# Memory reused tile by tile behind an attention stage, with one expert's weights split ahead of its first products

## The chip, the core and the metric

The kernel runs on one core of a Trainium2 chip. A core has TensorE (PE, matrix products), VectorE (DVE), ScalarE (ACT), GpSimd (POOL) and SyncE (SP), which here only issues transfers. The engines run beside each other and wait for each other through semaphores; each executes its own list of instructions in order. SBUF is the memory they work in, PSUM the accumulators that PE writes, and DRAM is reached by DMA. The metric is the device time of one execution, in microseconds, as the median of three runs.

## The reference

Attention over 8 batches, 8 heads, 576 positions and head dimension 64, with a causal window of 32 for four heads and a dilated one (every fourth position, 32 of them) for the other four; its 4608 x 512 output x then goes through a mixture of experts with one expert for each row:

```python
attn = softmax(where(mask, q @ k.T / 8, -1e9)) @ v      # window 32 | dilation 4
x = attn.transpose(0, 2, 1, 3).reshape(4608, 512)
logits = x @ w_gate                                     # 8 experts
e = argmax(logits, axis=1)
out[i] = gate[i] * (relu(x[i] @ w1[e[i]]) @ w2[e[i]])   # w1 512x1024, w2 1024x512
```

## The kernel before

**Attention** goes in 36 steps of 128 rows, nine for each of four pairs of batches; a step n runs scores of tile n, the weighted sum (`st_av`) of tile n-2, the transposes of tile n-3 (`st_xt`, copied by `st_xcopy`) and the logits of three tiles at a time (`st_logits`, `st_keep`). Its accumulators are the PSUM pool `psa` with tags X, S0, S1, T, O and L; its SBUF pools are `fix`, `ap`, `sp` and `late`. The ring buffers `qkr` and `vr` for q, k and v lie in `fix`. Finished rows are written to a DRAM table `x_d`.

**Routing** (`route(m)`) runs once for each pair of batches, as short pieces that the steps pull from a list (`on_pe`, `off_pe`). It transposes the logits (`turn`), takes the best expert of each row, counts with three small products (`rank`) how many rows each expert had before, and selects each row's place (`select`): a block of 128 slots and a slot in it. For the first three pairs POOL scatters the row numbers into three DRAM tables, 27 scatters in all; `read_table` reads these back into `t_in`. For the last pair the table is made on chip: for each of its nine tiles DVE writes `b1` (which of 320 blocks, L562) and `s1` (which slot, times the row number, L554), six buffers of each, and PE multiplies them into one accumulator `tb` (`enter`, L573). The sum of `tb` and the three tables is `row_i`, the row number for each slot of each expert; with it POOL gathers rows of `x_d`. In the listing POOL adds the three tables (L674, L675), and three DVE operations make `row_i` from them and `tb` (L656, L660, L661; the trace has the last as L437).

**The first expert** is partly ahead. Its first 256 rows come from the first two pairs, are gathered and transposed during attention, and `early_layer1` makes hidden blocks 0 to 3 of its first layer in attention's accumulators S0 and S1 while the last routing runs. Every weight unit (128 x 1024) is loaded into one of three `raw` buffers and split (`split_unit`): ACT writes the high part (L720), DVE the rest (L721). Units 0 to 3 (first layer) are ready early; units 4 to 6 (second layer) are loaded early and split later.

**Behind attention** `att.close()` releases its pools, and `ps`, `ph`, `pw1`, `pw2`, `px1`, `pd` and `py` are laid over their memory. A tile of such a pool waits for every user of the pools it is laid over. Then come `layer1` for hidden blocks 4 to 7, each 12 matmuls of 256 columns with ACT's `h` (L911) and DVE's (L912) behind it, and the split of units 4 to 7 (unit 7 is loaded only now, as a `raw` buffer must be free). From here the order of all engines is written out by hand: `keep_rows` (`row_i` to DRAM), the gathers of the first expert's other two blocks r0 and r1 and of the next expert's, the loads of the next expert's units (`bring`), `layer2` of the first expert's two blocks, `r0.prep_x` (four transposes, L970, of the gathered rows), `r0.layer1` (L1005), and so on for seven more experts. Up to that point from step 35 on the order is a scheduler's: it lists, for each engine, what is ready by its own estimates of time, first what stands first in the program, or what is marked with high priority.

Of the kernel before, what the change touches and what calls it, by code (L numbers as in the profile page):

```python
# [9 lines left out]
F32 = mybir.dt.float32  # L10
# [15 lines left out]
NE = 8  # L26
# [38 lines left out]
C_ID, C_TRI, C_REV, C_C0, C_NEW, C_IO, C_ATT = np.cumsum(  # L65
    [0, P, P, NE, NE, NE * NT, P]
).tolist()
C_ONE, C_BASE, C_THR, C_PU, C_D, C_P, C_BK, C_FIRST, C_WSTEP, C_UP, C_AT, C_ALL = (
    C_ATT + np.cumsum([0, P, NE, NTHR, NE, DBLK, DBLK, NBK, 2 * NE + 1, 2 * NE, 1, DBLK])
).tolist()  # L70


def _constants():
    c = np.zeros((P, C_ALL), np.float32)
    c[:, C_ID : C_ID + P] = np.eye(P)
    c[:, C_TRI : C_TRI + P] = -np.tril(np.ones((P, P)))
    c[:, C_ONE : C_ONE + P] = 1.0
    c[:, C_REV : C_REV + NE] = np.arange(NE, 0, -1)
    c[0, C_C0 : C_C0 + NE] = np.arange(NE) * CAP
    c[:, C_BASE : C_BASE + NE] = np.arange(NE) * CAP  # L80
    c[:, C_THR : C_THR + NTHR] = SLOTS + P * np.arange(NTHR)
    c[:, C_PU : C_PU + NE] = np.arange(NE)[None, :] * P + np.arange(P)[:, None]
    c[:, C_D : C_D + DBIG] = np.arange(DBIG)
    c[:, C_D + DBIG : C_D + DBLK] = np.arange(DTAIL)
    c[:, C_FIRST : C_FIRST + 2 * NE] = np.tile(np.arange(NE) * CAP + SLOTS, 2)
    c[:, C_FIRST + 2 * NE] = 2.0**20
    c[:, C_WSTEP : C_WSTEP + 2 * NE] = np.diff(np.append(np.tile(np.arange(NE), 2), NE - 1)) * 8 * P
    c[:, C_UP] = np.arange(P) // TAIL
    own = np.repeat(np.arange(P)[:, None], DBLK, 1)
    own[:, DBIG:] %= TAIL  # L90
    c[:, C_P : C_P + DBLK] = own
    c[:, C_AT : C_AT + DBLK] = own * (NBK + 1)
    c[:, C_NEW : C_NEW + NE * NT] = np.arange(NE * NT) % NT != 0
    c[:, C_IO : C_IO + P] = np.arange(P)
    c[:, C_BK : C_BK + NBK] = P * np.arange(NBK)
    row = (
        DUMMY
        + np.arange(NPR)[None, :, None] * S2
        + np.arange(NT)[None, None, :] * P
        + np.arange(P)[:, None, None]  # L100
    )
    tok = row[:, :-1].astype(np.int32)
    end = row[:, -1].astype(np.float32) - LAST

    t, p, w = np.meshgrid(np.arange(NT), np.arange(P), np.arange(KB), indexing="ij")
    q, k = P * t + p, P * t + p // QB * QB - W + w

    def near(n):
        return (k >= 0) & (q >= k) & (q - k < W) & (q // n == k // n)

    def blocks(m):
        m = m.reshape(-1, NB, QB, KB).transpose(2, 0, 1, 3).reshape(QB, -1)
        return np.where(m, 0.0, -BIG)


    mask = np.zeros((P, QB + NT * NB * KB), np.float32)
    mask[:QB, : QB + 3 * NB * KB] = np.concatenate(
        [np.eye(QB), blocks(near(S)[[0, S // P, 1]])], axis=1
    )
    mask[QB:] = np.concatenate([np.eye(QB), blocks(near(CLS))], axis=1)  # L120
    mask = mask.astype(mybir.dt.np(BF16))
    slots = np.repeat(np.arange(P, dtype=np.int32)[:, None], NBK, 1)
    return dict(cst=c, tok=tok, end=end, slots=slots, mask=mask, zero=np.zeros((DUMMY, XP), np.float32))
# [39 lines left out]
def attention_moe_kernel(ctx, tc, qk, v, wg, w, cst, tok, end, slots, mask, zero, out):  # L163
# [33 lines left out]
    t_in = [late.tile([P, NBK], I32, name=f"t_in{i}") for i in range(3)]  # L197

    NRQ, NRV = 6, 6
    qkr = fix.tile([P, NRQ, QK], F32, name="qkr")  # L200
    vr = fix.tile([P, NRV, VC], F32, name="vr")
    rows_i = fix.tile([P, NPR - 1, NT], I32, name="rows_i")
    rows_f = fix.tile([P, NT], F32, name="rows_f")
    wgz = fix.tile([P, 4, 32], F32, name="wgz")
# [228 lines left out]
    def on_pe(f, *a, late=False):  # L433
        side.append((2 if late else 1, lambda: f(*a)))

    def off_pe(f, *a, **k):
        side.append((0, lambda: f(*a, **k)))  # L437
# [15 lines left out]
    def hold(on):  # L453
        held_[0] = on
# [19 lines left out]
    def route(m, then=None, after=None):  # L474
# [25 lines left out]
        def small(name, shape=(P, NT, NE), dt=F32):  # L500
            return sp.tile(list(shape), dt, name=name, bufs=1)
# [7 lines left out]
        pos, blk_i, plc_i, at_i = [  # L509
            small(n, (P, NT), I32) for n in ("pos", "blk_i", "plc_i", "at_i")  # L510
        ]
        wide, pay = [small(n, (P, NT)) for n in ("wide", "pay")]
        load = small("load", (P, NT), I32)
        many = small("many", (P, NT, XP - DM))
        posf = small("posf", (P, NT))
# [35 lines left out]
        def mark(t):  # L551
            s1 = sp.tile([P, P], F32R, name="s1", bufs=6)
            b1 = sp.tile([P, NBK], F32R, name="b1", bufs=6)
            v.tensor_scalar(  # L554
                s1,
                ca[:, C_IO - C_TRI : C_IO + P - C_TRI],
                plc[:, t : t + 1],
                pay[:, t : t + 1],
                op0=ALU.is_equal,
                op1=ALU.mult,  # L560
            )
            v.tensor_scalar(  # L562
                b1, cc[:, C_BK - C_ATT : C_BK + NBK - C_ATT], blk[:, t : t + 1], None, op0=ALU.is_equal
            )
            hot[t] = s1, b1
# [47 lines left out]
        )  # L613
        if m == NPR - 2:
            off_pe(hold, True)
        on_pe(rank, late=True)
        off_both(
            select,
            lambda: v.tensor_reduce(
# [23 lines left out]
        else:  # L643
            off_both(
                lambda: v.tensor_copy(blk, blk_i),
                lambda: v.tensor_copy(plc, plc_i),
                lambda: v.tensor_tensor(pay, rows_f, plc, op=ALU.subtract),
            )
            off_pe(lambda: v.tensor_tensor(crun, crun, cs[:, :, NT - 1], op=ALU.add))
            for lo in range(0, NT + 3, 3):  # L650
                for t in range(lo, min(lo + 3, NT)):
                    off_pe(mark, t)
                if lo:
                    on_pe(enter, range(lo - 3, lo), late=True)
            off_pe(
                lambda: v.tensor_scalar(  # L656
                    scr, box["tb"], 0.0, float(LAST), op0=ALU.is_gt, op1=ALU.mult
                )
            )
            off_pe(lambda: v.tensor_tensor(scr, box["tb"], scr, op=ALU.add))  # L660
            off_pe(v.tensor_tensor, row_i, t_in[0], scr, op=ALU.add)  # L661
        if after:
            after()

# [6 lines left out]
    def add_tables(rows, n):  # L671

        t0, t1, t2 = [t[:, :n] for t in t_in]
        nc.gpsimd.tensor_tensor(t0, t0, t1, op=ALU.add)  # L674
        nc.gpsimd.tensor_tensor(rows, t0, t2, op=ALU.add)  # L675
# [451 lines left out]
    def at(n, f, *a):  # L1127
        todo.setdefault(n, []).append(lambda: f(*a))
# [2 lines left out]

    def read_all():
        read_table(NBK)
        add_tables(t_in[0], NBK)

    def early_fetch():
        def fetch():
# [27 lines left out]
        at(8 + 2 * u, early_split, u)  # L1165
    for u in range(4, 7):
        at(total + u - 4, early_load, u)

    def early_layer1(f):
        n = first.ns  # L1170
# [6 lines left out]
    def go(f, n):  # L1177
        if 0 <= n < total:
            f(n)
# [5 lines left out]
    def step(n):  # L1185
# [36 lines left out]
        pull_off()  # L1222
        go(st_logits, n - 4)
        go(st_keep, n - 4)
        pull_pe(late=True)
        go(st_mask, n + 1)
        if spare:
# [22 lines left out]
    att.close()  # L1250


    pools["ps"] = ctx.enter_context(tc.tile_pool(name="ps", bufs=2, space=PSUM))
    for key, bufs in (("h", 9), ("w1", 4), ("w2", 4), ("x1", 1), ("d", 1), ("y", 2)):
        pools[key] = ctx.enter_context(tc.tile_pool(name="p" + key, bufs=bufs))
    pools["w", 1], pools["w", 2], pools["x", 1] = pools["w1"], pools["w2"], pools["x1"]

    NJ = 2 * NE

# [169 lines left out]

    st_, nx = statics[0], statics[1]  # L1430
    a, c = 0, 2
    for f in range(4, 8):
        st_.layer1([f])
        raw = early.pop(f) if f in early else st_.load(f)
        st_.units.append(split_unit(1, raw))
    r0, r1 = rest0
    with tc.manual_schedule(engines=ENGS | {mybir.EngineType.Pool, mybir.EngineType.SP}):
        ahead = nx.ahead
# [21 lines left out]
        nx.fetch(1)  # L1460
        for u in range(3):
            bring(u)
        st_.layer2(0, range(6))
        some(3)
        st_.layer2(1, range(6))
        some(5)
        r0.prep_x()
        nx.fetch(2)
# [222 lines left out]
```

## Time and profile before

| | |
|---|---|
| median of three runs | 606.92 us (606.56 to 608.8) |
| the profiled execution | 606.45 us |
| its span, from the first instruction to the last | 604.7 us |
| PE, DVE, ACT, POOL busy | 97%, 60%, 52%, 31% |
| attention and routing, by the trace | about 0 to 187 us |
| experts, by the trace | about 165 to 599 us |

Times in the rows are from the span's start. A busy PE is not PE at its peak: matmuls overlap, and the end of each is modelled, so how fast PE really goes is read from the steps between starts. What ended an idle time stands in brackets behind the row.

### The profile page before, as it was taken

To read this page: it belongs to the slowest core of one execution; us is meant where nothing else is said; L and a number is where in the kernel's file an instruction comes from. 1 tells how busy PE (TensorE), PEld (TensorE's weight loads), DVE (VectorE), ACT (ScalarE), POOL (GpSimd) and SP (SyncE) were. 2 spreads that over 40 slices of the span, in tenths; PEclk is the share of its full clock that TensorE was granted. 3 is DMA by queue.
4 is the path that set the end of the run, shared out by engine and by line. 5 is a ranking of instruction groups with operands and counts; after the bars stand their busy time and mean duration, and the time that the engine had idled before them with its cause. 6 is when DMAs were issued, how large, how long until landed. Compare 5 with 4: busy or idle time off the path is not lost. (4 is left out here: it accounts for less than half of the span.)

```text
span 604.7 us, 13500 instructions
## 1 busy us (share of the span) xinstructions
PE 585.5 (97%) x5175; PEld 478.7 (79%) x5175; DVE 363.6 (60%) x786; ACT 315.3 (52%) x612; POOL 188.3 (31%) x234
## 2 busy tenths in 40 slices
PE   7999999999989999999999999999999999999995
PEld 6877778777777888888888888888888888888784
DVE  3877888887758457636564566457547646663200
ACT  2568776766723555534555466456536554662210
POOL 0346676486573225140033022202300330031011
PEclk8999999999999999999999999999999999999998
DMA  8999999995325538985778679778868786779411
GB/s 333 409 372 412 411 406 408 398 344 162 86 56 176 186 130 278 244 272 171 206 256 298 176 250 296 239 201 288 265 223 241 253 306 173 236 260 405 177 42 46
DMA packets 67522, 152.52 MB, mean 252 GB/s; under 512 B 15040, under 2 KB 31360, under 8 KB 67424
## 3 DMA queue, kind: packets, MB, share of 16 engines
q1 hardware_dynamic: 55744, 121.50, 59.5%
q0 software_dynamic: 11712, 30.14, 14.1%
q8 instruction: 41, 0.67, 0.5%
q14 instruction: 25, 0.20, 0.1%
HBM read 124.02 MB, written 28.60 MB: 252 GB/s over the span
## 5 line engine op out<-in xcount | busy, mean ns | idle before, releaser
L931 PE MATMUL yps<-wu,h 128*128 128x512 f32 x696 | 164.4, 392 | 0.0
L721 DVE TENSOR_TENSOR wu<-raw,wu 128x512 fp32r<-128x512 f32 x200 | 128.3, 687 | 55.7 <-ACT wu L720 49.9
L900 PE MATMUL hps<-x,wu 128*128 128x512 f32 (+1 forms) x720 | 161.6, 383 | 0.2 <-DVE h L912 0.2
L900 PEld LDWEIGHTS hps<-x,wu 128*128 128x128 f32 x720 | 132.3, 188 | 27.4 <-DVE h L912 0.8
L931 PEld LDWEIGHTS yps<-wu,h 128*128 128x128 f32 x696 | 129.4, 188 | 27.4 <-issue 0.6
L720 ACT CAST wu<-raw 128x512 fp32r<-128x512 f32 x200 | 112.9, 618 | 12.2 <-DMA raw<-in_w_dram 11.9
L796 POOL DMA_INDIRECT out_dram<-y,rows_all x30 | 30.4, 1012 | 197.8 <-ACT y L795 85.2
L912 DVE SCALAR_TENSOR_TENSOR h<-hps,h 128x512 fp32r<-128x512 f32 (+1 forms) x60 | 40.2, 671 | 52.4 <-ACT h L911 51.1
L911 ACT ACTIVATE h<-hps 128x512 fp32r<-128x512 f32 (+1 forms) x60 | 35.0, 583 | 62.5 <-PE hps L900 49.6
L323 ACT COPY pts<-pt 96x512 f32<-96x512 f32 x72 | 41.9, 582 | 46.9 <-PE pt L318 40.3
L746 POOL DMA_INDIRECT xg<-x_d,rows_all x30 | 32.0, 1065 | 95.0 <-DVE x L791 35.3
L297 DVE TENSOR_REDUCE nm<-s 128x4 f32<-128x384 f32 x72 | 39.7, 552 | 25.7 <-PE s L286 20.7
L318 PE MATMUL pt<-ident,p 128*96 128x128 f32 x288 | 47.5, 289 | 4.9 <-ACT pts L323 4.2
L795 ACT ACTIVATE y<-yps,gate 128x512 f32<-128x512 f32 x30 | 20.7, 688 | 45.5 <-PE yps L931 37.1
L333 PEld LDWEIGHTS o<-vr,pts 96*64 96x64 f32 x1152 | 37.9, 139 | 7.2 <-issue 6.1
L333 PE MATMUL o<-vr,pts 96*64 96x65 f32 x1152 | 43.1, 226 | 0.4 <-issue 0.4
L302 DVE TENSOR_TENSOR d<-s,nm 128x384 f32<-128x384 f32 x72 | 40.1, 557 | 4.6
L312 ACT ACTIVATE p<-d 128x384 f32<-128x384 f32 x72 | 37.6, 524 | 6.5 <-DVE d L302 6.5
L1037 PE MATMUL ypd<-wu,hd 128*128 128x512 f32 x168 | 40.7, 391 | 0.0
L365 POOL DMA_DIRECT2D x_d<-xs x36 | 20.6, 571 | 63.0 <-DVE xs L353 25.7
L1005 PE MATMUL hpd<-wu,xd 128*128 128x512 f32 x168 | 39.9, 391 | 0.0
L318 PEld LDWEIGHTS pt<-ident,p 128*96 128x96 f32 x288 | 28.9, 128 | 13.0 <-ACT pts L323 5.3
(161 smaller groups left out, 627.0 us busy)
## 6 DMA issues: line engine op xcount, KB each, us to landing
raw<-in_w_dram SPq DMA_DIRECT2D x104, 512.0 KB
qkr<-in_qk_dram SPq DMA_DIRECT2D x36, 576.0 KB
vr<-in_v_dram SPq DMA_DIRECT2D x36, 520.0 KB
rows<-xg SPq DMA_DIRECT2D x29, 264.0 KB
xg<-rows SPq DMA_DIRECT2D x116, 64.0 KB
wu<-in_w_dram SPq DMA_DIRECT2D x12, 512.0 KB
x_d<-xs POOLq DMA_DIRECT2D x44, 128.0 KB
wz<-in_w_dram SPq DMA_DIRECT2D x4, 512.0 KB
```

The lines of the kernel that those rows point to most:

```text
L297: nc.vector.tensor_reduce(st["nm", n][:, g], st["s", n][g], axis=AX.X, op=ALU.max)
L302: nc.vector.tensor_tensor(st["d", n][:, g], st["s", n][g], st["nm", n][:, g].broadcast_to([P, HP, KB]), op=ALU.subtract,)
L318: nc.tensor.transpose(pt[:KB, h], st["p", n][:, g, h], ident)
L323: nc.scalar.copy(st["pts", n][:, g], st.pop(("pt", n))[:KB])
L333: nc.tensor.matmul(st["o", n][QB * j : QB * (j + 1), g, h], lhsT=pts[:, g, h, QB * j : QB * (j + 1)], rhs=vr[:KB, n % NRV, a : a + DH + 1] ...
L720: nc.scalar.copy(u[:, 0, sl], raw[:, sl])
L721: nc.vector.tensor_tensor(u[:, 1, sl], raw[:, sl], u[:, 0, sl].bitcast(F32), op=ALU.subtract)
L900: nc.tensor.matmul(hps[:, : self.ns], lhsT=u[:, wpart, fs], rhs=self.x[:, xpart, c, : self.ns], start=(k == 0), stop=(k == 11),)
L912: nc.vector.scalar_tensor_tensor(h[:, 1, :n], hps[:, :n], 0.0, h[:, 0, :n].bitcast(F32), op0=ALU.max, op1=ALU.subtract,)
L931: nc.tensor.matmul(yps, lhsT=self.h[f][:, hpart, ts], rhs=u[:, wpart, fs], start=f == 0 and k == 0, stop=f == 7 and k == 2,)
L1005: nc.tensor.matmul(hps, lhsT=self.x[:, xpart, c], rhs=u[:, wpart, ns], start=(k == 0), stop=(k == 11),)
L1037: nc.tensor.matmul(self.yps, lhsT=self.h[f // 4][:, hpart, f % 4], rhs=u[:, wpart, fs], start=f == 0 and k == 0, stop=f == 7 and k == 2,)
```

## The change

1. `qkr` and `vr` move to a pool `ring` of their own on the other side of SBUF; it is closed after attention's last weighted sum, and `pw1` is opened on its bytes.
2. `pw1`, `ps`, `ph`, `pw2`, `px1`, `pd` and `py` get `reuse_waits="tile"`: a tile waits only for the earlier tiles on its own bytes (in PSUM, its own bank).
3. Units 4 to 6 of the first expert are split in steps 38 and 39 instead of behind attention (`second_split`).
4. `layer1` of hidden blocks 4 to 7 gets high priority as one group, and so do the last pair's `rank` and the operations that end the table.
5. POOL's two additions of the tables go; DVE adds the three tables itself, five operations in a row (`rows_out`).
6. `s1` takes the row number from `rows_f` and leaves out the subtraction of the slot (`pay` goes); the slot comes in later through a constant of each partition.
7. The hold on the third pair's `rank` ends in step 35.
8. `layer2` of the two blocks runs hidden blocks 0 to 3 of both first, then 4 and 5 of both.

```diff
-    qkr = fix.tile([P, NRQ, QK], F32, name="qkr")
-    vr = fix.tile([P, NRV, VC], F32, name="vr")
+    ring = ExitStack()
+    ringp = ring.enter_context(tc.tile_pool(name="ring", bufs=1, side="right"))
+    qkr = ringp.tile([P, NRQ, QK], F32, name="qkr")
+    vr = ringp.tile([P, NRV, VC], F32, name="vr")
...
         def mark(t):
...
-            v.tensor_scalar(
+            v.scalar_tensor_tensor(
                 s1,
                 ca[:, C_IO - C_TRI : C_IO + P - C_TRI],
                 plc[:, t : t + 1],
-                pay[:, t : t + 1],
+                rows_f[:, t : t + 1].broadcast_to([P, P]),
...
-        on_pe(rank, late=True)
+        if m < NPR - 1:
+            on_pe(rank, late=True)
+        else:
+
+            def rank_first():
+                with tc.high_priority():
+                    rank()
+
+            on_pe(rank_first, late=True)
...
-                lambda: v.tensor_tensor(pay, rows_f, plc, op=ALU.subtract),
...
-            off_pe(
-                lambda: v.tensor_scalar(
-                    scr, box["tb"], 0.0, float(LAST), op0=ALU.is_gt, op1=ALU.mult
-                )
-            )
-            off_pe(lambda: v.tensor_tensor(scr, box["tb"], scr, op=ALU.add))
-            off_pe(v.tensor_tensor, row_i, t_in[0], scr, op=ALU.add)
+
+            def rows_out():
+                with tc.high_priority():
+                    v.tensor_scalar(
+                        scr,
+                        box["tb"],
+                        0.0,
+                        cc[:, C_LP - C_ATT : C_LP + 1 - C_ATT],
+                        op0=ALU.is_gt,
+                        op1=ALU.mult,
+                    )
+                    v.tensor_tensor(scr, box["tb"], scr, op=ALU.add)
+                    v.tensor_tensor(scr, t_in[0], scr, op=ALU.add)
+                    v.tensor_tensor(scr, t_in[1], scr, op=ALU.add)
+                    v.tensor_tensor(row_i, t_in[2], scr, op=ALU.add)
+
+            off_pe(rows_out)
...
     def read_all():
         read_table(NBK)
-        add_tables(t_in[0], NBK)
...
+    def second_pool():
+        ring.close()
+        pools["w", 1] = pools["w1"] = ctx.enter_context(
+            tc.tile_pool(name="pw1", bufs=4, side="right", reuse_waits="tile")
+        )
+
+    def second_split(u):
+        first.units.append(split_unit(1, early.pop(u)))
+
+    at(total + 1, second_pool)
+    for u in range(4, 7):
+        at(total + 2 + (u - 4) // 2, second_split, u)
...
+        if n == total - 1:
+            hold(False)
         pull_pe(late=True)
...
-    pools["ps"] = ctx.enter_context(tc.tile_pool(name="ps", bufs=2, space=PSUM))
-    for key, bufs in (("h", 9), ("w1", 4), ("w2", 4), ("x1", 1), ("d", 1), ("y", 2)):
-        pools[key] = ctx.enter_context(tc.tile_pool(name="p" + key, bufs=bufs))
+    pools["ps"] = ctx.enter_context(
+        tc.tile_pool(name="ps", bufs=2, space=PSUM, reuse_waits="tile")
+    )
+    for key, bufs in (("h", 9), ("w2", 4), ("x1", 1), ("d", 1), ("y", 2)):
+        pools[key] = ctx.enter_context(
+            tc.tile_pool(name="p" + key, bufs=bufs, reuse_waits="tile")
+        )
...
-    for f in range(4, 8):
-        st_.layer1([f])
-        raw = early.pop(f) if f in early else st_.load(f)
-        st_.units.append(split_unit(1, raw))
+    with tc.high_priority():
+        st_.layer1(range(4, 8))
+    st_.units.append(split_unit(1, st_.load(7)))
...
-        st_.layer2(0, range(6))
+        st_.layer2(0, range(4))
+        st_.layer2(1, range(4))
         some(3)
-        st_.layer2(1, range(6))
+        st_.layer2(0, range(4, 6))
+        st_.layer2(1, range(4, 6))
```

## Rows read from the trace of the kernel before

**Rows 1.** Busy time and count of each engine by stretch; granted clock, DMA.

```profile
163.00:174.67 11.67, 11.40 (x117) 10.10 (x117) 6.67 (x37) 5.52 (x14) 9.46 (x14) 1.00 0.23 70
174.67:179.22 4.55, 2.42 (x20) 2.21 (x18) 2.93 (x16) 0.00 (x0) 3.85 (x4) 1.00 0.10 18
179.22:184.91 5.69, 4.59 (x28) 3.69 (x28) 5.49 (x17) 0.90 (x3) 2.06 (x2) 1.00 0.34 88
400.00:500.00 100.00, 100.00 (x450) 82.76 (x449) 60.59 (x95) 55.49 (x99) 21.54 (x20) 1.00 0.79 254
```

**Rows 2.** Who waited for whom, 172 to 190 us: total, times, longest.

```profile
ACT h L911 <- DVE s L554: 10.0, 1, 10.0
...
DVE sel L530 <- PE rk L526: 1.6, 1, 1.6
```

**Rows 3.** PE's instructions by time: start, duration, line, count, wait.

```profile
166.91 1.68 PE L900 MATMUL s<-x,wu 128*128 128x256 f32 x12
168.51 0.85 PE L401 MATMUL ps_l<-xt,wgz 128*32 128x384 f32 x8
...
174.67 2.42 PE L900 MATMUL hps<-x,wu 128*128 128x256 f32 x18
179.22 0.42 PE L573 MATMUL tb<-b,s 128*128 128x320 f32 x1 [2.13 <-DVE s L554]
...
195.37 0.60 PE L970 MATMUL tpx<-ident,xg 128*128 128x128 f32 x4
...
197.21 2.90 PE L1005 MATMUL hpd<-wu,xd 128*128 128x512 f32 x12
```

**Rows 4.** DVE's instructions by time.

```profile
173.13 0.23 DVE L585 SCALAR_TENSOR_TENSOR cand<-sh,ca 128x72 f32<-128x72 f32 x1
...
178.11 0.15 DVE L647 TENSOR_TENSOR pay<-rows_f,plc 128x9 f32<-128x9 f32 x1
...
180.25 0.33 DVE L554 TENSOR_SCALAR s<-ca,plc,pay 128x128 fp32r<-128x128 f32 x1
...
180.81 0.90 DVE L554 TENSOR_SCALAR s<-ca,plc,pay 128x128 fp32r<-128x128 f32 x1
...
184.43 0.42 DVE L912 SCALAR_TENSOR_TENSOR h<-hps,h 128x256 fp32r<-128x256 f32 x1 [0.20 <-ACT h L911]
184.77 0.48 DVE L656 TENSOR_SCALAR scr<-tb 128x320 f32<-128x320 f32 x1
185.16 0.68 DVE L721 TENSOR_TENSOR wu<-raw,wu 128x512 fp32r<-128x512 f32 x1
185.76 0.48 DVE L660 TENSOR_TENSOR scr<-tb,scr 128x320 f32<-128x320 f32 x1
...
186.76 0.48 DVE L437 TENSOR_TENSOR rows_all<-t_in,scr 128x320 int32<-128x320 int32 x1
```

**Rows 5.** POOL's instructions by time.

```profile
180.59 1.03 POOL L674 TENSOR_TENSOR t_in<-t_in,t_in 128x320 int32<-128x320 int32 x1 [1.46 <-DMA t_in<-tab]
...
187.53 1.54 POOL L746 DMA_INDIRECT xg<-x_d,rows_all  x1 [4.24 <-DVE rows_all L437]
...
221.11 1.10 POOL L746 DMA_INDIRECT xg<-x_d,rows_all  x1 [0.31 <-issue]
```

**Rows 6.** SP's issues by time.

```profile
187.30 0.38 SPq L679 DMA_DIRECT2D table<-rows_all  x1
...
225.64 3.39 SPq L758 DMA_DIRECT2D rows<-xg  x2
```

**Rows 7.** DMA queues from 187.2 to 193 us: packets, MB, share of engines.

```profile
q0 software_dynamic: 72, 0.25, 22.5%
```

**Rows 8.** Stretches at the start: PE busy, clock.

```profile
8.00:10.00 2.00, 1.05 (x34) 0.81 (x36) 1.21 (x3) 1.05 (x2) 0.00 (x0) 1.00 1.00 406
10.00:11.00 1.00, 1.00 (x18) 0.75 (x9) 0.56 (x1) 0.00 (x0) 0.00 (x0) 0.58 1.07 424
16.00:17.00 1.00, 1.00 (x22) 1.00 (x22) 0.97 (x3) 0.48 (x1) 0.00 (x0) 0.51 0.99 392
```

More of the change, by code (lines that the diff above doesn't have):

```diff
@@ L67 @@
 ).tolist()
-C_ONE, C_BASE, C_THR, C_PU, C_D, C_P, C_BK, C_FIRST, C_WSTEP, C_UP, C_AT, C_ALL = (
-    C_ATT + np.cumsum([0, P, NE, NTHR, NE, DBLK, DBLK, NBK, 2 * NE + 1, 2 * NE, 1, DBLK])
+C_ONE, C_BASE, C_THR, C_PU, C_D, C_P, C_BK, C_FIRST, C_WSTEP, C_UP, C_AT, C_LP, C_ALL = (
+    C_ATT + np.cumsum([0, P, NE, NTHR, NE, DBLK, DBLK, NBK, 2 * NE + 1, 2 * NE, 1, DBLK, 1])
 ).tolist()
@@ L92, in _constants @@
     c[:, C_AT : C_AT + DBLK] = own * (NBK + 1)
+    c[:, C_LP] = LAST - np.arange(P)
     c[:, C_NEW : C_NEW + NE * NT] = np.arange(NE * NT) % NT != 0
@@ L511, in route @@
         ]
-        wide, pay = [small(n, (P, NT)) for n in ("wide", "pay")]
+        wide = small("wide", (P, NT))
         load = small("load", (P, NT), I32)
@@ L1250, in attention_moe_kernel @@
     att.close()
-    pools["ps"] = ctx.enter_context(tc.tile_pool(name="ps", bufs=2, space=PSUM))
-    for key, bufs in (("h", 9), ("w1", 4), ("w2", 4), ("x1", 1), ("d", 1), ("y", 2)):
-        pools[key] = ctx.enter_context(tc.tile_pool(name="p" + key, bufs=bufs))
-    pools["w", 1], pools["w", 2], pools["x", 1] = pools["w1"], pools["w2"], pools["x1"]
+    pools["ps"] = ctx.enter_context(
[5 more added lines that the diff above has]
+        )
+    pools["w", 2], pools["x", 1] = pools["w2"], pools["x1"]
     NJ = 2 * NE
```

## The prediction

> **What bounds the kernel now.** Four views were read. The share of each engine says PE (97%), and the stretches say the same for most of the run: from 400 to 500 us PE starts 450 matmuls of 512 columns, 0.222 us each, without a gap [rows 1]. There the change alters nothing, so its worth is what it gives PE back where PE does starve. The stretches show one such place, the passage from attention to the first expert: in 174.67:179.22 PE is busy 2.42 of 4.55 us, in 179.22:184.91 the 28 matmuls are short ones that wait in between [rows 1]. The list of waits names why: ACT's first `h` stood 10.0 us behind the last `s1` (L554), the last reader of attention's pools, and with it hidden block 7, whose accumulator block 4 holds [rows 2].
>
> How much PE could get back is read from its timeline between its first matmul for hidden block 4 at 174.67 and the transposes of r0's gathered rows at 195.37, 20.7 us [rows 3]. In it lie 48 matmuls of 256 columns (18 in 2.42, the last 0.28 long: (2.42 - 0.28) / 17 = 0.126 each, 6.0), 36 of 512 columns of `layer2` (0.222, 8.0), nine of 320 columns for the table (about 0.15, an estimate between the two, 1.4) and 0.1 of counts: 15.5. So 5.2 us are lost, 0.86% of the run, and no version of this change gives more.
>
> **What is late next.** The transposes need r0's rows, and these hang on a chain that PE's work does not shorten: logits, `rank`, the marks, `row_i` at 187.24 (186.76 + 0.48) [rows 4], POOL's gather at 187.53 [rows 5], landing. A gather moves 128 rows of 2112 bytes, 0.27 MB; POOL's queue had moved 0.25 MB by 193.0 [rows 7]. So r0 landed after 193.0 and before 195.37, 5.8 to 8.1 us behind `row_i`; I take 6.9, 194.1. PE's own work and that landing end within about a microsecond of each other now. Freeing PE alone therefore gains at most about 1 us; the rest moves to a wait for r0. Whether `row_i` or the landing comes earlier decides.
>
> **Part by part, for the time of `row_i`.**
>
> *Tile waits and high priority for `layer1`.* Hidden block 4's accumulator, the first of its tag, should lie in the bank of attention's first tag, X. By tiles it waits only for the copy of the last X tile (behind the transposes that precede 166.91); before, it waited for all of attention's accumulators, to 174.67. With high priority its 12 matmuls (12 x 0.126 = 1.5) then go in front of what is left of the hidden block at 166.91 and of the logits at 168.51 [rows 3]. PE loses nothing, but the routing chain behind the logits is 1.5 us later. Bounds: 0 (the scheduler puts the logits first) and 1.5; I take 1.5, as the priority says so.
>
> *`rank` first.* It had its place already; what came late was `select`, 1.6 us behind it with PE full of matmuls [rows 2]. What held it I can't read. 0 to 1.4 earlier; I take half, 0.7.
>
> *POOL's additions go.* While they run, a mark takes 0.90 us (180.81) instead of 0.33 (180.25); there are two such [rows 4, 5]: 1.1 earlier. The Trainium skill (GPSIMD Engine Reference, Key points) has the mechanism: GpSimd shares its SBUF interfaces with VectorE. The trace agrees, with 0.90 against 0.33.
>
> *`s1` with two tensors.* `pay` goes, 0.15 [rows 4]. An operation of the new kind took 0.23 at 72 columns and 0.42 at 256, so by a straight line 0.29 at 128, no more than the 0.33 of now [rows 4]: nothing. The Trainium skill (VectorE: DVE Perf Modes, What auto-detection actually checks) speaks against this edit: fp32 takes the double rate with a single source only. By it nine marks of 128 columns would lose some 0.6 us, an estimate from that page; the rows give no sign of it, and the sum goes by the rows.
>
> *DVE's h parts move into the marks.* Blocks 5 and 6 now get their `h` while the marks run: two at about 0.35 (184.43 to the next start, 184.77) [rows 4], 0.7 later. Bounds 0 and, with a late split between, 1.6.
>
> *The end of the table.* Now three operations with two splits between them, 184.77 to 187.24, 2.5 us, of which the splits take 2 x 0.60 (185.16 to 185.76) [rows 4]. Then five in a row at about 0.5: 2.5. No change.
>
> Sum: 187.24 + 1.5 - 0.7 - 1.1 - 0.15 + 0.7 = 187.5. With all the good ends 184.6, with all the bad ones 189.1.
>
> *What costs nothing.* Splitting units 4 to 6 early is six operations of some 0.6 us on each of ACT and DVE, 3.6, and lies under 163 to 174.67, where ACT is busy 5.52 and DVE 6.67 of 11.67 us [rows 1]; without that cover each would hold a routing step for up to 0.7. The load of unit 7 then comes early too. On SP only `keep_rows` (187.30 [rows 6]) stands behind it and waits for `row_i` as now; the next expert's three loads follow it at once, where now they wait for buffers. So POOL's gather meets three loads in the DMA engines instead of one or two. The third pair's `rank` half a step earlier and the new order of `layer2` move no work; the order only means that 24 matmuls, 5.3 us, need neither unit 6 nor block 4's `h`.
>
> *Block 4's `h`.* It is the first tile of the pool that begins where `fix` began, so on the bytes of `rows_f` and `ca`, which every mark reads. So it should wait for the last mark even tile by tile, and then stand behind the table's five operations on DVE: `h` at about 187.9, block 7 (1.5) to 189.4, twelve matmuls of `layer2` (2.7) to 192.1. That is when PE is through.
>
> **The forecast.** r0 lands at 187.5 + 6.9 = 194.4, 2.3 us behind PE; the transposes start at about 194.6 instead of 195.37. From there all runs as before, 0.8 us earlier. The profiled execution took 606.45: 605.65; the median of the runs stands 0.47 above it: 606.1 us, 0.1% less.
>
> **The rivals.**
>
> 1. *The chain gets short and the gather quick (faster).* `select` is prompt and the logits are not held up: `row_i` near 185. The gather at 221.11 was followed by its store at 225.64 [rows 5, 6], 4.5 us, so a gather can land earlier than 5.8. At 185.3 + 4.5 = 189.8 PE's own work decides, 15.5 us from 174.67, with a microsecond for the pace of the marks: 191.2. Gain 4.2, 602.7; with one of the two alone about 604. For it: 1.4 us of unexplained wait. Against: in the stretch in question the gather did not land in 5.8 us, and it gets more company. The Trainium skill (DMA: Bandwidth & Descriptors, Queues, rings and completion order) says that a DMA engine goes round between its queues packet by packet, so that a gather would wait for little of the loads; by that rule this rival holds. The trace does not agree so far, with 0.25 MB in the 5.5 us behind the issue.
>
> 2. *The clock falls (slower).* PE has so far no long wait in one piece: the longest is 2.13 us (179.22), at full clock [rows 1, 3]. With the change it may stand still from 192.1 to r0's landing. At the start, after stretches in which PE was busy 1.05 of 2.00 us, the granted clock fell to about 0.5 (1.2 GHz) in 10:11 and stayed to 17, some 6.6 us [rows 8]. Such a stretch in the dense part costs half of it, 3.3 us: 609.4 with the forecast's landing, over the line of 0.5% as soon as r0 lands 0.5 us later. For it: the wait is new and near the longest seen. Against: 2.13 us left the clock alone.
>
> 3. *The change doesn't do what it says (the same).* Block 4's `h`, and with it ACT's list, stays behind the last mark, and no block goes in front of the logits: `row_i` 1 us earlier at most, 606 to 607.
>
> **Chances and range.** Forecast 0.54, rival 1 0.22, rival 2 0.12, rival 3 0.12. What a measurement of this kernel can tell from no change is about 0.5%, 3.0 us. Faster by more: most of rival 1 and a little of the forecast's low end, 0.21. Slower by more: most of rival 2, 0.09. Within: 0.70. The forecast's own range goes from `row_i` at 186.3 to 188.7 and the landing 6.2 to 7.7 behind it: 604.4 to 608.1. The range for 8 in 10 reaches into rivals 1 and 2: 603.0 to 609.0.
>
> **What would show it.** In the profile of the changed kernel: 12 matmuls of block 4 before the logits, near 168; `row_i` between 186.3 and 188.7; marks at 0.33 throughout; L720 and L721 of units 4 to 6 before 172; PE idle one to three microseconds in front of L970, released by the gather; granted clock 1.00 there. If L970 starts before 192, the landing, not the chain, was mis-sized; if `row_i` comes before 185, the chain was; if the clock shows 0.5 near 195, rival 2 has it.

## The result, and the profile after

The changed kernel took 612.3 us (median of ten runs, 608.7 to 614.0); the kernel before, run beside it, 608.61 (ten runs, 606.56 to 611.03). The ratio is 1.0063, 95% interval 1.0045 to 1.008: slower by 0.6%. The forecast's 606.1 started from a kernel before of 606.92 (three runs); the 1.7 us up to 608.61 aren't the change's. The profiled execution took 610.64 us with a span of 608.9, against 606.45 and 604.7 before.

Where the 4.2 us of span went is read by cutting both traces at three marks of TensorE: the start of unit 33's weighted sum, the last of the early transposes of gathered rows, and the last tail product.

| | start to unit 33 | passage | experts | tail |
|---|---|---|---|---|
| before | 156.46 | 60.38 | 369.81 | 18.03 |
| after | 157.09 | 60.66 | 373.06 | 18.05 |
| difference | +0.63 | +0.28 | **+3.25** | +0.02 |

Three quarters of the loss lie among the experts, where the change seems to touch nothing. The second of these rows by stretch answers to the last of [rows 1]: 445 matmul starts in 100 us, 450 before, at the same full clock (columns: length; busy time and count of PE, PEld, DVE, ACT, POOL; clock; DMA). The first is the end of the passage, where PE is busy 6.79 of 8.57 us.

```profile
187.70:196.27 8.57, 6.79 (x33) 5.29 (x31) 4.13 (x12) 0.39 (x1) 3.87 (x4) 1.00 0.62 194
400.00:500.00 100.00, 100.00 (x445) 81.73 (x444) 60.33 (x95) 54.72 (x98) 20.80 (x19) 1.00 0.81 249
```

The timeline shows which matmuls are slower. Expert 2's first layer is one row of 96 matmuls. This is the row in the kernel before:

```profile
268.10 21.92 PE L900 MATMUL hps<-x,wu 128*128 128x512 f32 x96
```

In the changed kernel (next row) it is 0.64 us longer: its steps are 0.229 to 0.236 us, 0.2333 in the mean, where before all are 0.226 to 0.227, 0.2267 in the mean. Expert 5's row is the same; these are the two experts whose whole first layer takes its weights from `pw1`, the pool that the change moves to the other side of SBUF (three such pools go round).

```profile
269.08 22.56 PE L920 MATMUL hps<-x,wu 128*128 128x512 f32 x96
```

The two rows make 1.28 of the 3.25 us. The rest is taken up in the experiments.

In the passage, PE's timeline answers to [rows 3]:

```profile
164.51 1.16 PE L336 MATMUL o<-vr,pts 96*64 96x65 f32 x32
165.60 0.66 PE L388 MATMUL tp<-ident,xs 128*128 128x128 f32 x4
166.01 1.55 PE L920 MATMUL s<-x,wu 128*128 128x256 f32 x11
...
170.56 0.85 PE L404 MATMUL ps_l<-xt,wgz 128*32 128x384 f32 x8
...
176.18 0.87 PE L920 MATMUL hps<-x,wu 128*128 128x256 f32 x6
178.00 0.44 PE L528 MATMUL rk<-oh,ca 128*128 128x72 f32 x2 [0.96 <-DVE oh L592]
...
182.15 1.66 PE L576 MATMUL tb<-b,s 128*128 128x320 f32 x5
...
191.48 3.01 PE L951 MATMUL yps<-wu,h 128*128 128x512 f32 x12
196.27 0.63 PE L990 MATMUL tpx<-ident,xg 128*128 128x128 f32 x4 [1.78 <-DMA xg<-x_d,rows_all]
```

PE is through at 194.5 and then waits 1.78 us for r0's rows. DVE's timeline answers to [rows 4]; the first row is the last tile's `z` in the kernel before, all others are of the changed kernel:

```profile
165.09 0.16 DVE L343 TENSOR_SCALAR z<-o 128x8 f32<-128x8 f32 x1
...
167.26 0.17 DVE L346 TENSOR_SCALAR z<-o 128x8 f32<-128x8 f32 x1 [3.36 <-PE tp L388]
...
174.20 0.69 DVE L741 TENSOR_TENSOR wu<-raw,wu 128x512 fp32r<-128x512 f32 x1 [0.36 <-ACT wu L740]
...
175.47 0.68 DVE L741 TENSOR_TENSOR wu<-raw,wu 128x512 fp32r<-128x512 f32 x1
176.07 0.22 DVE L584 TENSOR_REDUCE mx<-lt 128x9 f32<-128x72 f32 x1
...
178.82 0.23 DVE L533 TENSOR_TENSOR sel<-rk,oh 128x72 f32<-128x72 f32 x1 [0.25 <-issue]
...
184.93 0.34 DVE L557 SCALAR_TENSOR_TENSOR s<-ca,plc,rows_f 128x128 fp32r<-128x128 f32 x1
...
185.72 0.42 DVE L932 SCALAR_TENSOR_TENSOR h<-hps,h 128x256 fp32r<-128x256 f32 x1 [0.15 <-ACT h L931]
186.14 0.55 DVE L668 TENSOR_SCALAR scr<-tb,cc 128x320 f32<-128x320 f32 x1
186.61 0.41 DVE L932 SCALAR_TENSOR_TENSOR h<-hps,h 128x256 fp32r<-128x256 f32 x1
186.94 0.48 DVE L676 TENSOR_TENSOR scr<-tb,scr 128x320 f32<-128x320 f32 x1
187.34 0.41 DVE L932 SCALAR_TENSOR_TENSOR h<-hps,h 128x256 fp32r<-128x256 f32 x1
187.67 0.48 DVE L677 TENSOR_TENSOR scr<-t_in,scr 128x320 f32<-128x320 int32 x1
188.45 0.42 DVE L932 SCALAR_TENSOR_TENSOR h<-hps,h 128x256 fp32r<-128x256 f32 x1 [0.30 <-ACT h L931]
188.79 0.48 DVE L678 TENSOR_TENSOR scr<-t_in,scr 128x320 f32<-128x320 int32 x1
189.30 0.49 DVE L679 TENSOR_TENSOR rows_all<-t_in,scr 128x320 int32<-128x320 int32 x1
```

Three things stand on the chain to `row_i` that were not there: `z` of the last tile starts 1.59 us behind the end of its products (164.51 + 1.16 = 165.67) while PE streams on, where before it was 0.40; two halves of a split (L741) stand among the last logits' reductions; and of four `h` halves one goes ahead of the five operations that end the table and three between them. Gone are the late `select` (now 0.04 us behind the end of `rank`, before 1.52) and the marks of 0.90 us. In the list of waits, which answers to [rows 2], ACT's `h` of block 4 still stands behind the last mark:

```profile
POOL xg L766 <- DVE rows_all L679: 9.4, 1, 9.4
ACT h L931 <- DVE s L557: 8.4, 1, 8.4
```

The chain, link by link, in us from unit 33's weighted sum:

| link | before | after | forecast, difference | measured |
|---|---|---|---|---|
| to the logits | 12.05 | 13.47 | +1.5 | +1.42 |
| to the maximum `mx` | 4.09 | 5.51 | 0 | +1.42 |
| to `select` | 3.72 | 2.75 | -0.7 | -0.97 |
| to the first mark | 1.30 | 1.23 | -0.15 | -0.07 |
| to the end of the last mark | 6.60 | 5.52 | -1.1 + 0.7 | -1.08 |
| to the end of `row_i` | 3.03 | 4.22 | 0 | +1.19 |
| to r0's transposes | 8.12 | 6.48 | | -1.64 |

### The profile page after: what moved, and what is told of

The parts are those of the page before. It is cut to its first block, busy times and chain, and to the rows that moved or that the text cites. A ratio compares the mean times of both kernels' runs of the same rounds, so it can differ in the third digit from the quotient of the medians.

```text
span 608.9 us, 13481 instructions
## 1 busy us (share of the span) xinstructions
PE 588.4 (97%) x5175; PEld 478.5 (79%) x5175; DVE 363.9 (60%) x787; ACT 315.7 (52%) x612; POOL 186.0 (31%) x232
## 5 line engine op out<-in xcount | busy, mean ns | idle before, releaser
L741 DVE TENSOR_TENSOR wu<-raw,wu 128x512 fp32r<-128x512 f32 x200 | 128.2, 686 | 59.0 <-ACT wu L740 50.5
```

What stands on the lines that cost most here:

```text
L741: nc.vector.tensor_tensor(u[:, 1, sl], raw[:, sl], u[:, 0, sl].bitcast(F32), op=ALU.subtract)
```

## The experiments

Each group of kernels ran in one session (close together in time, on one chip) beside the kernel before, whose median there is named, since it differs between the sessions (602.62 to 607.95). Two of the four sessions, with 607.8 and 602.75 us, name the same chip number, so that the chip makes this difference is not shown. Profiled executions, one for each kernel, are cut at the marks of the first table. In all of them the granted clock is 1.00 in the passage.

**Where w1 lies: three kernels.** The layout puts `w1` at byte 131744 of a partition before, at 196576 after. Within 1024 bytes that is 672 and 992, within 256 bytes 160 and 224. `w1_high` moves the pool up and keeps its place within 1024:

```diff
-    for key, bufs in (("h", 9), ("w1", 4), ("w2", 4), ("x1", 1), ("d", 1), ("y", 2)):
+    for key, bufs in (("h", 9), ("w2", 4), ("x1", 1), ("d", 1), ("y", 2), ("w1", 4)):
```

> The kernel before with one edit: the pool of the first-layer weights (w1) is opened last, so that it lies at the top of SBUF, at byte 193184 of a partition instead of 131744, and the pools behind it move down by its 32 KiB. Its place within 1024 bytes stays that of before (672). Theory A (height: w1 is read more slowly by the matmuls because it lies high in SBUF): the expert stage loses what the changed kernel lost there, about 3 us, so 609.5 to 612 us, and the matmuls of expert 2's and expert 5's first layer start 0.2333 us apart. Theory B (alignment: the place within 1024 bytes, 992 instead of 672, is what slows): as before within 0.5%, steps of 0.2267 us throughout. Theory C (neither; the slower steps come from the traffic of another order of loads): as before too.

`w1_high_off` puts a tile of 320 bytes ahead of it:

```diff
+    if key == "pad":
+        gap = pools[key].tile([P, 80], F32, name="gap")
+        nc.gpsimd.memset(gap, 0.0)
```

> As w1_high, and with 320 bytes of padding ahead of w1, so that it begins at byte 193504, 992 within 1024, the place within 1024 that it has in the changed kernel. Theory A (height): 609.5 to 612 us, as w1_high. Theory B (alignment): 609.5 to 612 us, steps of 0.2333 us in expert 2's and expert 5's first layer, while w1_high stays as before. Theory C (order of loads): as before, 606.5 to 609 us. The difference between this run and w1_high is what 320 bytes of shift do.

`after_pad` does the reverse to the changed kernel:

```diff
+    padp = ctx.enter_context(tc.tile_pool(name="padp", bufs=1, side="right"))
+    gap = padp.tile([P, 80], F32, name="gap")
+    nc.gpsimd.memset(gap, 0.0)
     ring = ExitStack()
```

> The changed kernel with 320 bytes of padding at the right end of SBUF, so that w1 lies at byte 196256 instead of 196576 and its place within 1024 bytes is 672, that of before. Nothing else differs. Theory B (alignment): the expert stage gives back its 3 us, steps of 0.2267 us in every expert, and some 0.9 us of loss (what the passage from attention to the experts lost) is left: 607 to 608.5 us in a profile like that of before. Theory A (height) and theory C (order of loads): as the changed kernel, 610 to 612.5 us.

The kernel before took 602.62 us beside these three. `w1_high` took 603.7 (ratio 1.0023, 1.0001 to 1.0045), `w1_high_off` 606.07 (1.0067, 1.0042 to 1.0092), `after_pad` 604.87 (1.0044, 1.0018 to 1.0071). Expert 2's first layer in PE's timeline, `w1_high`, then `w1_high_off`, then `after_pad`:

```profile
265.02 21.92 PE L900 MATMUL hps<-x,wu 128*128 128x512 f32 x96
```

```profile
264.51 22.56 PE L900 MATMUL hps<-x,wu 128*128 128x512 f32 x96
```

```profile
265.35 21.92 PE L923 MATMUL hps<-x,wu 128*128 128x512 f32 x96
```

The same height gives both times, and 320 bytes switch between them in either direction: theory A (height) and theory C (order of loads) fall, theory B (alignment) stands. The expert stage took 369.22, 371.38 and 369.43 us.

So 320 bytes cost 2.2 us of the expert stage, and 2.4 us by the medians of `w1_high` and `w1_high_off`. Cut at each change of operands, the expert stage gives the same: 1.28 us in the two layers, and 0.02 to 0.12 us in each of some twenty other groups of matmuls, alike in all four profiles with `w1` at 224 within 256 (the changed kernel's two, `w1_high_off`, and `shift_64` below), 2.4 us together. Of the other 0.9 of the changed kernel's 3.25 us nearly all is in three groups in which also kernels with a fast `w1` differ among each other (0.45 in expert 6's first layer, 0.27 and 0.11 in two short ones); the stages of those kernels reach from 369.0 to 371.1 us. What makes this scatter is open.

By its median `after_pad` keeps more of its loss than the 0.9 us that theory B left it: 2.2 us (1.1 to 4.3 by the interval), where its profiled execution stands 0.7 above `w1_high`'s (spans of 602.0 and 601.3).

**Which alignment: four kernels, one execution each.** `pads_a` gives each of the four buffers a pool of its own behind 32 bytes; the `shift` kernels are `w1_high_off` with 64, 128 and 256 bytes in place of 320.

> w1_high with its four w1 buffers in four pools of one buffer, each behind 32 bytes of padding, so that the buffers lie 32, 64, 96 and 128 bytes behind their places there: 64, 96, 0 and 32 within 128 bytes. In expert 2's and expert 5's first layer the 24 matmuls of each buffer show its step. Theory B1 (the place within 128 bytes decides): 0.2333 us for the second buffer alone if 96 is the only slow place, for others too if 0 or 64 are slow as well, 0.2267 us for the fourth. Theory B2 (the place within 256, 512 or 1024 bytes decides): the fourth buffer may be slow, and which of the others are need not follow 128.

> w1_high with 64 bytes of padding ahead of w1 (320 there slowed expert 2's and expert 5's first layer from 0.2267 to 0.2333 us a matmul). All four buffers move alike. If the place within 128 bytes decides, slow, as with 320, which leaves the same rest: expert stage 371 to 373 us from the last of the early transposes to the last tail matmuls, against 369.2 to 370.6 in the fast places. If a longer stretch decides (256 bytes: 320 leaves 64 as well, so slow too; 512 or 1024: then 64 may be fast).

> As shift_64 with 128 bytes. Place within 128 bytes decides: fast, 0.2267 us a matmul, expert stage 369.2 to 370.6 us. Place within 256 or more decides: may be slow, 0.23 us or more.

> As shift_64 with 256 bytes. Place within 128 or 256 bytes decides: fast, 0.2267 us, 369.2 to 370.6 us. Place within 512 or 1024 decides: slow if 320 was slow by its 256 and not by its 64.

The same row in `shift_64`, `shift_128` and `shift_256`:

```profile
271.42 22.56 PE L900 MATMUL hps<-x,wu 128*128 128x512 f32 x96
```

```profile
268.34 22.48 PE L900 MATMUL hps<-x,wu 128*128 128x512 f32 x96
```

```profile
269.55 21.92 PE L900 MATMUL hps<-x,wu 128*128 128x512 f32 x96
```

The expert stages took 372.03, 372.81 and 370.25 us, the executions 611.93, 609.81 and 608.41 beside 607.8. So shifts of 0 and 256 are fast, 64, 128 and 320 (64 over 256) slow: the place within 256 bytes fits all of them, and the reading by 128 falls. In `pads_a` (one execution, 608.51 us beside 607.95) the row took 22.42 us, and all four buffers were slow, the one at +128 as well; steps next to each other mix two buffers, so it gives no step for one buffer alone. In the layouts of all these kernels the pools of x, `h`, `w2` and the first weights lie at 160 within 256, so whether place 160 itself counts, or the same place as the other operand's, is not separated. With what the weights collide at 64 and 128 wasn't tried.

**The early end of the hold.** `after_hold` is `after_pad` without item 7 of the change:

```diff
-        if n == total - 1:
-            hold(False)
         pull_pe(late=True)
```

> after_pad without the early end of the hold at the last unit (the two lines ahead of the pull for TensorE in the last part). Theory D: the early end lets block 4's other work in front of the last attention unit's z and transposes, so that the chain to row_i starts about 1 us late; without it row_i ends near 188.5 us instead of 189.8 and r0's first transposes start about 1 us earlier: 0.5 to 1 us less than after_pad. Theory E: the late start is a late signal of TensorE that has nothing to do with the hold: row_i near 189.8, time as after_pad within 0.3%.

604.5 us beside 602.62 (1.0033, 1.0012 to 1.0054). Against `after_pad`, `row_i` ends 1.03 us earlier, but unit 33 already starts 1.02 earlier, so nothing of that is the hold's: from unit 33 to r0's transposes it is 37.47 us against 37.61. In `after_pad` `z` followed its products at once, so theory E's late signal wasn't there to be tested; it was in the changed kernel's own profile, in another session. So the changed kernel was run again:

> The changed kernel once more, on another chip and beside the kernel before. If its slowness is the matmul step in w1's place and some chance waits in the passage: 0.3 to 0.8% slower, expert stage 372 to 373.5 us from the last early transposes to the last tail matmuls, steps of 0.2333 us in expert 2's and expert 5's first layer; the passage from unit 33's values to the last early transposes 59 to 60.7 us, by whether the signal for the last z comes late again (it came 1.6 us after its matmul in the first profile).

610.69 us beside 607.8 (1.0048, 1.0023 to 1.0073), experts 372.32, and the wait is there again, 1.56 us behind the products:

```profile
166.88 0.17 DVE L346 TENSOR_SCALAR z<-o 128x8 f32<-128x8 f32 x1 [3.33 <-PE tp L388]
```

In the sessions where the kernel before takes 607 to 609 us, `z` was late in 2 of 2 profiles with the early end and in none of 8 without it (six of them of kernels with before's attention order). In those of 602.6 to 602.8 us it was late in none of 8, one of them (`after_pad`) with the early end. No slow session had a pair of kernels that differ in the early end alone, so that it makes `z` late is likely but not shown. `select` behaves alike: with before's order, in the slower sessions, 0.77 to 1.56 us late in 5 of 6 and 0.10 in the sixth; on time (0.04 at most) in both profiles of a quicker session and in all ten profiles with the change's `rank` order. So TensorE's signal came up to 1.6 us late while it streamed matmuls, in some sessions and behind certain orders. Why is open.

**The rings' place alone.** `before_ring` is the kernel before with item 1's rings on the other side:

```diff
-    qkr = fix.tile([P, NRQ, QK], F32, name="qkr")
+    qkr = ringp.tile([P, NRQ, QK], F32, name="qkr")
...
+    ring.close()
     att.close()
```

> The kernel before with one part of the change alone: the rings of queries, keys and values lie in a pool of their own on the other side of SBUF, closed where attention ends, so the expert stage's pools lie where they did. Theory H (the rings' new place costs attention some 0.8 us, as the profiles of the changed kernels against those of the kernels with before's attention suggest on each chip, 157.1 against 156.5 and 154.0 to 155.0 against 153.1 to 153.9 at unit 33's values): 0.5 to 1.5 us slower than before. Theory J (that is the scatter of single executions): ratio 1.000 within 0.002.

609.56 us beside 607.95 (1.0032, 1.0013 to 1.0051), 0.8 to 3.1 us: J falls, H's bounds are within reach. But its profile reached unit 33 at 157.20, 1.06 us behind `pads_a` in that session, with half of that lost in one unit, and lost another 1.6 us in the passage (61.95). Other kernels of that session with the rings there reached unit 33 at 156.72 and 156.80. In another session three kernels with before's rings reached it at 156.65 to 156.88 and the changed kernel at 156.74, and four kernels that share the changed kernel's rings scatter from 152.77 to 155.27. So the cost isn't located, and that the rings' place slows attention is not shown.

**The loads ahead of the gather.** `loads`: `after_hold` with the next expert's first two units ahead of `keep_rows`, and unit 7's load issued with the early ones.

```diff
         nx.begin()
+        for u in range(2):
+            bring(u)
         keep_rows()
...
-        for u in range(3):
-            bring(u)
+        bring(2)
```

> after_hold with the weight loads of expert 1's units 0 and 1 ahead of the table's reads and of keep_rows on SP's queue, where their buffers come free some 15 us earlier (units 4 and 5 are split by then). Theory F: the gather for r0 lands 6.3 us after row_i in the changed kernel because these two loads share its stretch (DMA share 0.96 to 0.99 in the five microseconds ahead of r0's transposes); in front of it they use a stretch with a share of 0.01 to 0.4, the gather lands 3.5 to 4.5 us after row_i, and TensorE's wait of 1.75 us ahead of r0's transposes is gone: 1 to 1.8 us less than after_hold. Rival G: the landing takes its 6 us by itself; the wait stays and the time is after_hold's within 0.3%.

606.05 us beside 607.95 (0.9973, 0.9953 to 0.9993). From unit 33 to r0's transposes 36.73 us, 0.74 less than `after_hold`; the landing came down from 6.37 to 5.67 us behind `row_i`, and the wait is shorter but still there:

```profile
193.45 0.63 PE L993 MATMUL tpx<-ident,xg 128*128 128x128 f32 x4 [1.05 <-DMA xg<-x_d,rows_all]
```

Theory F's size falls (3.5 to 4.5 us): the loads cost 0.7 us of the landing, and most of it is the gather's own, as rival G had it. G's other half, the time of `after_hold` within 0.3%, can't be told, as the two ran in different sessions.

**The chain's two new pieces.** `hold_sums` and `hold_split` undo one each on `after_hold`; `hold_both` both; `combo` both with `loads`. The sums (GpSimd as before) and the split:

```diff
         read_table(NBK)
+        add_tables(t_in[0], NBK)
...
                     v.tensor_tensor(scr, box["tb"], scr, op=ALU.add)
-                    v.tensor_tensor(scr, t_in[0], scr, op=ALU.add)
-                    v.tensor_tensor(scr, t_in[1], scr, op=ALU.add)
-                    v.tensor_tensor(row_i, t_in[2], scr, op=ALU.add)
+                    v.tensor_tensor(row_i, t_in[0], scr, op=ALU.add)
```

```diff
-    st_.units.append(split_unit(1, st_.load(7)))
+    raw7 = st_.load(7)
...
         some(3)
+        st_.units.append(split_unit(1, raw7))
+        bring(2)
```

> loads, and two parts of the change undone: GpSimd sums the two further tables again, as before, so that three operations instead of five close the chain on VectorE, and the split of unit 7 of expert 0 goes behind row_i, so that its two VectorE halves (0.68 us each) no longer stand among the reductions of the last logits. Expected if these are what made row_i late (3.0 us later than in the kernel before against the same start of the passage): row_i 1.1 us earlier by the split, 1.0 to 1.8 us by the sums, TensorE's wait of 0.96 us ahead of the rank's products gone, in all 1 to 2 us less than loads, and 0.2 to 0.6% faster than the kernel before. If TensorE's own work bounds the passage by then: as loads within 0.5 us.

> after_hold with GpSimd summing the two further tables as before, so that three operations instead of five stand between the last mark and row_i. From the end of the last mark to the end of row_i after_hold took 4.21 us, two of its operations (0.48 us each) with the halves of h between them (0.41 us each). Theory K (VectorE's sums are on the path): 2.5 to 3.0 us, as in the kernel before, row_i 1.2 to 1.7 us earlier against the same start; r0's transposes follow, 1 to 1.7 us earlier. Theory L (the prediction's step: GpSimd's sums end so late that row_i waits for them): 3.5 to 4.2 us, no gain.

> after_hold with the split of unit 7 behind row_i on VectorE and nothing else moved but the load that waits for its buffer. Theory M (two halves of 0.68 us stand on the chain among the last logits' reductions): from the end of the last logits' turn to the first mark 1.3 us less than after_hold's 5.5 us, so 4.1 to 4.3 us, TensorE's wait of 0.96 us ahead of the rank's products gone, row_i and r0's transposes 1.0 to 1.3 us earlier. Rival N (the halves fill time in which VectorE would wait for ScalarE and TensorE): 5.0 to 5.5 us and no more than 0.3 us.

> hold_sums and hold_split together, without combo's earlier loads. If the earlier loads were what held up GpSimd's scatters in combo (two stalls of 1.2 and 1.8 us ahead of them, the sums 1 us late): row_i 1 us earlier than combo's against the same start, the gather lands 6.3 us after row_i instead of 5.7, r0's transposes within 0.5 us of combo's, time as combo within 0.3%, 0.3 to 0.7% faster than the kernel before. If the earlier loads are worth more than that: 1 us slower than combo.

> combo once more beside hold_both, on whatever chip this is: 0.3 to 0.8% faster than the kernel before; passage from unit 33's values to the last early transposes 56.3 to 57.2 us.

One profile each; `hold_sums`, `hold_split`, `hold_both` and `combo_again` are of a session of 602.75 us:

| us | logits to `select` | last mark to `row_i` | unit 33 to `row_i` | unit 33 to r0's transposes | passage |
|---|---|---|---|---|---|
| after_hold | 7.77 | 4.21 | 31.10 | 37.47 | 58.95 |
| hold_sums | 7.99 | 3.19 | 29.83 | 38.10 | 59.57 |
| hold_split | 6.44 | 4.21 | 29.77 | 36.19 | 57.67 |
| hold_both | 6.53 | 2.52 | 28.70 | 35.48 | 56.94 |
| loads | 7.84 | 4.22 | 31.06 | 36.73 | 58.21 |
| combo | 6.54 | 3.64 | 29.44 | 35.18 | 56.63 |
| combo_again | 6.52 | 3.34 | 29.12 | 35.15 | 56.62 |

The split costs what theory M said: 1.3 us of the chain, and 1.28 us reach r0's transposes; rival N falls. In `hold_split`'s timeline of PE the wait ahead of the rank's products is 0.18 us, where the changed kernel has 0.96:

```profile
172.31 0.44 PE L531 MATMUL rk<-oh,ca 128*128 128x72 f32 x2 [0.18 <-DVE se L610]
...
190.82 0.63 PE L993 MATMUL tpx<-ident,xg 128*128 128x128 f32 x4 [1.12 <-DMA xg<-x_d,rows_all]
```

The sums are on the path too: `row_i` 1.27 us earlier, as theory K said. But alone this gained nothing, against K's second half: in `hold_sums` POOL issued the gather 1.25 us behind `row_i`, released by an `h` half of DVE's, and r0 came 0.63 us later than in `after_hold` (POOL's row, then PE's):

```profile
184.81 1.02 POOL L767 DMA_INDIRECT xg<-x_d,rows_all  x1 [1.77 <-DVE h L933]
```

```profile
191.83 0.63 PE L991 MATMUL tpx<-ident,xg 128*128 128x128 f32 x4 [2.63 <-DMA xg<-x_d,rows_all]
```

In `hold_both` and `combo` PE no longer waits for r0 at all; its own work ends last (PE's row of `combo`):

```profile
191.98 0.60 PE L991 MATMUL tpx<-ident,xg 128*128 128x128 f32 x4
```

So the earlier loads can bring little more there: 0.3 us (35.48 against 35.18). And `row_i` is later with them: in `combo` one of POOL's scatters waits for 1.80 us, and `row_i` 0.97 for POOL's second sum, where `hold_both` has neither wait (POOL's row first):

```profile
177.29 0.96 POOL L548 DMA_INDIRECT tab<-load,at_i  x1 [1.80 <-DMA tab<-load,at_i]
```

```profile
185.75 0.49 DVE L680 TENSOR_TENSOR rows_all<-t_in,scr 128x320 int32<-128x320 int32 x1 [0.97 <-POOL t_in L696]
```

**Do they beat both?** `combo` took 604.18 us beside 607.95 (0.9939, 0.9915 to 0.9963) in one session, and `combo_again` 603.26 beside 602.75 (0.9999, 0.9976 to 1.0021) in another, `hold_both` there 602.58 (0.9998, 0.9979 to 1.0017). `hold_sums` and `hold_split`, one execution each, took 602.43 and 603.76. So `combo` beats the kernel before in the session where that takes 608 us, and equals it in the one of 602.75. It did not run beside the changed kernel, which took 1.0048 and 1.0063 of the kernel before in sessions of 607.8 and 608.61. `combo_again`'s profiled execution, at 599.25 us, is the shortest of twelve that reach to 604.76; its passage is 3.2 us shorter than `w1_high`'s, the median is not. What the other executions lose, and the 2 us by which `after_pad` and `after_hold` stand above before, one profile each doesn't show; both stay open.

## Why the prediction was wrong

**The step that failed is the sentence "From there all runs as before, 0.8 us earlier".** The experts don't run as before: they take 3.25 us longer in the profiled execution and 2.5 in the second. Some 2.4 us of that are `w1`'s, which lies 64 bytes off its place within 256, so that the matmuls of two layers take 0.2333 us instead of 0.2267; 320 bytes of padding made this loss in one kernel and took it away in another. The forecast counted item 1 as a move of memory without a price and gave it no rival.

**The passage** was forecast 0.8 us shorter and came out 0.28 longer here (0.49 longer in the second profile), 1.3 shorter in `after_pad`, where no signal was late. Against `w1_high` of the same session, where none was late either, `after_pad`'s is 0.8 shorter (59.1 against 59.9), the forecast's number, but by luck: `row_i` comes 2.95 us later there (31.11 against 28.16 behind unit 33), not 0.3. Step by step, in the changed kernel's profile:

- *Block 4's matmuls in front of the logits, +1.5.* Wrong cause, right size. They start at 176.18, behind the logits. Of the +1.42, 1.19 are the late `z` (1.59 against 0.40), which was seen with item 7 only; the forecast said that item moves no work.
- *`rank` first, -0.7.* Right and larger: the late signal is gone (-1.49), and 0.5 of it goes to VectorE's other work that now stands in between (with unit 7's halves gone, in `hold_split`, that 0.5 is gone too). In `w1_high` `select` was on time without this item, so there was nothing to gain.
- *Splits cost nothing under the cover of 163 to 174.67.* Those of units 4 to 6 do: behind them DVE still waits 0.34 us for TensorE, at 173.59. Unit 7's, which the forecast saw coming early, was taken to cost nothing as well. Its two halves stand behind the cover and cost 1.3 us (`hold_split`), the price named for "without that cover".
- *POOL's additions, -1.1; `h` parts in the marks, +0.7.* The marks gained 1.08, 0.34 us each throughout. The `h` parts went behind the marks, between the table's operations.
- *Two tensors for `s1`: nothing.* Right: 0.34 us against 0.33. The Trainium skill (VectorE: DVE Perf Modes, What auto-detection actually checks) would have it some 0.6 us longer for the nine, as the forecast worked out; the runs don't show that.
- *The end of the table, 2.5 us, no change.* Wrong: 3.65 us from 186.14, as three `h` halves come between the five operations. With GpSimd's sums back and unit 7's split moved (`hold_both`) last mark to `row_i` takes 2.52 us, with the sums alone 3.19, instead of 4.21.
- *The landing, 6.9 us behind `row_i`.* 6.48 here, 6.37 in `after_hold`; a little long.
- *Block 4's `h` behind the last mark even tile by tile.* Right, 8.4 us of wait.
- *PE through at 192.1.* 194.5, as the chain behind the marks was 2.3 us later than forecast (189.79 against 187.5).

**The rivals.** Rival 1 (short chain, quick gather) is what `combo` comes near: r0's transposes 35.18 us behind unit 33 instead of 38.91, 3.7 us, with PE's own work deciding. But the gather alone was never seen to land within less than 5.4 us of its issue where PE waited for it (`loads`). By the rule that the forecast set beside it (the Trainium skill, DMA: Bandwidth & Descriptors, Queues, rings and completion order) the loads should hardly delay it; the 0.7 us of `loads` agree with that. Rival 2 (the clock falls; the fall at the start, taken as 6.6 us, is 6.8 by [rows 8], which changes its price by 0.1) didn't come: in `hold_sums` PE stood still for 2.63 us, and the clock stayed at 1.00, the 2.4 GHz level (columns as in the first fence):

```profile
189.20:191.83 2.63, 0.00 (x1) 0.04 (x1) 0.00 (x0) 0.00 (x0) 0.42 (x1) 1.00 1.03 411
191.83:196.00 4.17, 4.17 (x21) 3.50 (x22) 0.69 (x1) 1.37 (x3) 1.94 (x2) 1.00 0.41 131
```

## What to carry to other kernels

A pool that moves takes its alignment with it: compare the step between matmul starts per stage before and after any change of layout, and where it differs, pad the pool back to the place within 256 bytes that it had. Work that is "early" still has a place in each engine's list: look at which operations of the longest chain it stands in front of. And one profile can hold a wait that another session's doesn't have, so a passage is compared from a mark inside it, not from the start of the run.

## What the hardware showed

- A matmul of 512 columns with its weights at place 160 within 256 bytes stepped every 0.2267 us; with them 64 or 128 bytes further the mean step was 0.2333 and 0.232, at the full granted clock; 256 bytes further it was 0.2267 again. The pools of the other operands stayed at 160.
- TensorE's signal for finished products came up to 1.6 us late while it streamed on, at `z` or at `select`, in some sessions and not in others.
- A gather of 0.27 MB landed 5.4 to 7.0 us behind its issue wherever PE waited for it, and with two loads of 512 KB out of its way it was 0.7 us shorter (`loads` against `after_hold`).
